# Softmax sums beside a preset epsilon, one-instruction adds and minima along an axis, and a new table of order, in an attention, mixture and feed-forward chain

## The chip, the cores and the metric

The kernel runs on one core of one Trainium2 chip. The metric is the device time of one execution in microseconds (us). Before the change it was 473.57 us, the median of three runs (472.63 to 473.67).

## The reference, cut to what matters

Three layers follow one another. A windowed attention with 32 global rows (batch 4, 8 heads, 512 local and 32 global rows, head dimension 64) feeds four attention experts with a causal mask and a gate over the two best experts, and these feed a feed-forward block whose inputs are mixed with the row before. Every softmax divides by a sum to which 1e-9 is added:

```
def sm(s):
    s = s - np.max(s, axis=-1, keepdims=True)
    e = np.exp(s)
    return e / (np.sum(e, axis=-1, keepdims=True) + 1e-09)
s_g = scale * np.matmul(q_g, k_all.transpose(0, 1, 3, 2))
out_g = np.matmul(sm(s_g), v_all)
...
a_l = sm(s_l)
...
a = np.exp(scores)
a /= a.sum(-1, keepdims=True) + 1e-09
ye = a @ v @ wo[e]
```

## The kernel before, in words

The first stage (some 110 us) is the windowed attention. A step `n` is two heads by half of the local rows, 32 steps in all. `a_qk` (line 290) makes the scores of a step on TensorE (PE, tiles `S`). For each of the four pieces of a step VectorE (DVE) takes the row minimum of the negated scores while it adds the mask (tile `sm`, minimum in `mn`), and ScalarE (ACT) takes the exponential and adds up the rows into a column of `su` (line 316). `a_norm` (line 320) adds EPS to the four sums with a `tensor_scalar` into `rc`, takes the reciprocal, both on DVE, and GpSimd (POOL) multiplies the exponentials by it (tiles `pn`, `glob`). `a_tp` and `a_tg` transpose on PE (`pT`, `pTg`), and `a_pv` multiplies with the values on PE (tiles `x`). The 32 global rows of a batch go the same way in `g_qk`, `g_norm`, `g_tp` and `g_pv` (lines 367 to 422; tiles `Sga`, `Sgb`, `gl`, `pTG`, `pTh`, `xg`); there the minimum of two partial minima is a `tensor_tensor` (line 384), and `g_norm` adds EPS to one sum per half (line 392).

The second stage (to some 250 us) is the experts: projections `pv` and `pb`, scores `C` in `c_qk` (line 560), EPS and reciprocal in `c_norm` (line 581, tile `crc`), a multiplication by the gate and the scaling of `csm` on POOL, transposes `cT`, products `y`. The 32 last rows of a batch go through `l_qk` and `l_norm` (lines 610 and 629). The third stage multiplies the expert outputs with combined weights `G` (tiles `Gr`, `Gk`; `r00c` is the first product with them), then runs `k` and `v` to the end and stores.

Sums stand in small tiles of their own, `su` in 4 rotating buffers, `csu` in 3 and `sug` in 2, written with a step of two elements where a step has several.

Nothing is sent when it is called. `chain_kernel` records every operation in a list (class `Log`), and line 1052 sends them in the order of a table, ORDER: a string of steps, where `-3` goes back three places and `22x6` goes forward 22 and takes six operations in a row. Each engine works in that order, as do the DMA issues on the SP queue, and an instruction that waits holds up what stands behind it on its engine. SLOTS says which of its rotating buffers a tile takes. Both tables were made outside the kernel.

Of the kernel before, what the change touches and what calls it, by code (L numbers as in the profile page):

```python
# [18 lines left out]
S = SL + SG  # L19
# [100 lines left out]
def chain_kernel(ctx: ExitStack, tc: tile.TileContext, kq, vw, vgd, wqkv, wo, pack, w_k, w_v, w_r, c_causal, out):  # L120
# [30 lines left out]
    mu = small[:, SG + B + 144:SG + B + 144 + 2 * NC].rearrange("p (k c) -> p k c", k=2)  # L151
    zcol = tiny.tile([128, 1], F32, name="zcol")
# [137 lines left out]
    def a_qk(n):  # L290
# [29 lines left out]
    def a_norm(n):  # L320
# [6 lines left out]
        nc.vector.tensor_scalar(rc, su, EPS, None, op0=ALU.add)  # L327
# [39 lines left out]
    def g_qk(b):  # L367
# [9 lines left out]
        for h in range(2):  # L377
            t = pg[h]
            mn = T("mng", [4], f"mng{b}{h}", F32, 2)
            su = T("sug", [1], f"sug{b}{h}", F32, 2)  # L380
# [3 lines left out]
            nc.vector.tensor_tensor(mn[:, 2:3], mn[:, 0:1], mn[:, 1:2], op=ALU.min)  # L384
            nc.scalar.activation(t, t, AF.Exp, bias=mn[:, 2:3], scale=-1.0, accum_out=su)
            rs["g", b, h] = su

    def g_norm(b, h):
# [3 lines left out]
        nc.vector.tensor_scalar(rc, su, EPS, None, op0=ALU.add)  # L392
# [167 lines left out]
    def c_qk(b, ep, i):  # L560
# [5 lines left out]
        su = T("csu", [2, 2], f"csu{b}{ep}{i}", F32, 3)[:, :, 0]  # L566
# [4 lines left out]
        for e in range(2):  # L571
# [4 lines left out]
                                            accum_out=su[:, e:e + 1])  # L576
# [4 lines left out]
    def c_norm(b, ep, i):  # L581
# [3 lines left out]
        nc.vector.tensor_scalar(rc, su, EPS, None, op0=ALU.add)  # L585
# [24 lines left out]
    def l_qk(b):  # L610
# [8 lines left out]
        su = T("lsu", [1], f"lsu{b}", F32, 1)  # L619
# [6 lines left out]
        nc.scalar.activation(t[:, 0:S], t[:, 0:S], AF.Exp, bias=mn[:, 3:4], scale=-1.0, accum_out=su)  # L626
        crs["l", b] = su

    def l_norm(b):
# [4 lines left out]
        nc.vector.tensor_scalar(rc, su, EPS, None, op0=ALU.add)  # L634
# [420 lines left out]
def sequence(text):  # L1055
    n = 0
    for word in text.split():
# [8 lines left out]
0 10 -3 9 -19x2 22x6 -7 -15 7 -16 13 -12 -3 10 -11 16 -15 -2 4 3 -3 -2 585 -486 -95 65x8 -29x8 21 1 -2 2 -76 209x8  # L1066
-141 -4 -77 51 25 -25 65 -65 23 -23 438 -472x8 21 164 1 -164 101 64 -65 -106 -24 128 -124 -6x2 1 132 -119 110 -28x8 79
-182 -3 68 54 -55 -75 74 32x8 -143x8 21 113 -63 21 59 3x8 -11 -21 -131 150 32 -88x8 -111 190 -55 29 -94 83 -152 -6 -2
61 105 23 -56 -75 -61 71x8 56 121 -167 74 -33 -137 61 -61 174x4 31 -150 106 35 6 -175 141 32 -15 1 -163 -20 116 65 -54
-42 -47 74 171 -204 -68 45 -3 2 -47 172 44 295 -476 63x4 -106 547 -376 95 -124 -107 204x4 263 -444 180 -145 -56x4 196  # L1070
-230x4 1686 -1539 -120 -30 44 67x4 106 -107 36x32 338 -423 -86 226 -232 231 -206 -26 230 5x4 -214 447 -388 153 -32x8
22 1 230 -386 -5 92x8 -103 8 155x8 -175 9 100 -164 158 -18x2 -83 134 -195 189 -3 6 56x8 -168 70 -22 -50 70 27 -99 64
31 170x8 -215 33 72 -168 164 -99 75x4 24 -171 167 -72 -27 146x40 -112 -100 22 100x2 107 -212 103 207 -106 -205x4 91
174 -85 -83 101 -272x4 332 -282 320 -308 70x4 14 9 98 -16 -249 139 -47x4 65 -6 122x8 -40 -152 222 187 -172x8 165 -459
456 -189 -199 -76 70 50x32 -85 393 -388x2 -6x2 202 -199 -9 232 -225 217 -77 77 -146x2 145 -85 -138 121 -129 126 -121
133 32x8 -34 51 -31 -88 65 18 3 -21 -71 99x8 202 -192 -36 83x8 -87 -43 260 -218 -44 262 -204 -38x4 12 149 -153 26 196
-74 -174 49 -46 40 -149x5 193x4 180x12 -192 -95 1386 -1343 69 -3 -68 69 -6 325x12 -332 -38 26 178 -206 -76 107 3 -44
# [201 lines left out]
```

## Time and profile before

| | us |
|---|---|
| median of three runs | 473.57 |
| lowest and highest | 472.63, 473.67 |
| the profiled execution's own time | 474.15 |
| its span, first to last instruction | 472.4 |
| what lies around the span | 1.75 |

The profile is of one execution. Busy times are of instructions; a matmul's end is modelled, since matmuls are pipelined, so a busy PE isn't PE at its peak. The chain of waits is followed back from the last instruction: at each step to what released it, or to the instruction ahead of it on its engine. Idle time is put down to what ended it.

### The profile page before, as it was taken

Reading aid. Unit: us, or ns where it says so; the run is one execution under the profiler, and the core shown is the slowest. Engines: PE = TensorE matmul, PEld = TensorE weight load, DVE = VectorE, ACT = ScalarE, POOL = GpSimd, SP = SyncE. Lnnn points to the kernel's source line nnn. Section 1 sums busy time; section 2 is a strip of 40 time slices with the busy share of each in tenths; the row PEclk is TensorE's granted clock in tenths of the full one; section 3 lists DMA queues with packets and bytes.
Section 4 is the critical chain, followed back from the end, with each engine's and each line's share of the span. In section 5 each row is a group of like instructions: output and inputs, shape, how many; then the busy total and the mean of one; then the engine's idle time right before and its main releaser. Section 6 shows DMA issues by size and latency. Waiting matters only on the chain.

```text
span 472.4 us, 11799 instructions
## 1 busy us (share of the span) xinstructions
PE 460.1 (97%) x4226; PEld 394.4 (83%) x4226; DVE 340.8 (72%) x1170; ACT 293.7 (62%) x917; POOL 277.7 (59%) x439
## 2 busy tenths in 40 slices
PE   8799999999999999999999999999999999999996
PEld 6688788989997998897768768898888988889884
DVE  4799878967798577887799979999973652238512
ACT  5999899876767666777677867865440423215230
POOL 4989677486457777963897337665551244305450
PEclk9899999999999999999999999999999999999999
DMA  8978373201100000102121654422523500015003
GB/s 328 411 293 316 117 267 145 92 25 46 46 3 1 2 0 2 46 2 89 46 67 47 211 191 164 142 60 61 149 74 111 180 2 0 1 54 177 17 0 111
DMA packets 19701, 48.38 MB, mean 102 GB/s; under 512 B 2484, under 2 KB 3124, under 8 KB 19644
## 3 DMA queue, kind: packets, MB, share of 16 engines
q1 hardware_dynamic: 19356, 47.38, 29.8%
q8 instruction: 33, 0.54, 0.5%
q10 hardware_dynamic: 288, 0.26, 0.2%
q14 instruction: 24, 0.20, 0.1%
HBM read 38.70 MB, written 8.93 MB: 101 GB/s over the span
## 4 chain that ended last, share of the span: by engine, by line
PE 79%; DVE 7%; POOL 5%; ACT 4%; DMA 3%; issue 1%; ACTq 0%; POOLq 0%; DVEq 0%
PE v L107 20%; PE x L107 5%; PE pv L107 4%; PE S L107 4%; PE y L107 3%; PE C L107 3%; PE pT L107 3%; PE cT L107 3%; POOL csm L107 2%; PE Gr L107 1%; PE xg L107 1%; DVE csm L107 1%; DMA rawk<-in_moe_w_k_dram 1%; DMA rawv<-in_moe_w_v_dram 1%; ACT sm L107 1%
## 5 line engine op out<-in xcount | busy, mean ns | idle before, releaser
L107 PE MATMUL v<-wv,kk 128*128 128x512 f32 x408 | 99.3, 391 | 0.0
L107 PEld LDWEIGHTS v<-wv,kk 128*128 128x128 f32 x408 | 74.1, 188 | 13.7 <-POOL kk L107 0.2
L107 ACT ACTIVATE sm<-sm,mn 128x160 f32<-128x160 f32 x128 | 53.4, 421 | 7.4 <-DVE mn L107 7.3
L107 POOL TENSOR_TENSOR kk<-kb,kk 128x512 fp32r<-128x512 f32 (+3 forms) x40 | 34.7, 885 | 38.1 <-ACT kk L107 37.8
L107 POOL TENSOR_TENSOR csm<-csm,crc 128x512 f32<-128x512 f32 (+3 forms) x64 | 46.8, 752 | 1.2
L107 POOL TENSOR_TENSOR pn<-sm,rc 128x256 f32<-128x256 f32 x64 | 39.1, 631 | 13.2 <-DVE rc L107 8.6
L107 ACT ACTIVATE csm<-csm,cmn 128x384 f32<-128x384 f32 (+3 forms) x64 | 35.9, 562 | 15.4 <-DVE cmn L107 11.6
L107 DVE CUSTOM_DVE_ANT_0 sm<-S,band 128x160 f32<-128x160 f32 x128 | 35.6, 315 | 10.3 <-PE S L107 7.3
L107 POOL TENSOR_TENSOR kk<-kd,kk 128x256 fp32r<-128x256 f32 (+2 forms) x32 | 20.3, 644 | 36.8 <-ACT kk L107 36.8
L107 DVE CUSTOM_DVE_ANT_0 csm<-C,causal 128x384 f32<-128x384 f32 (+3 forms) x64 | 30.6, 485 | 8.3 <-PE cT L107 3.5
L107 DVE SCALAR_TENSOR_TENSOR kb<-kc,ks 128x256 f32<-128x256 f32 (+1 forms) x24 | 16.8, 699 | 21.0 <-ACT ks L107 17.2
L107 DVE TENSOR_TENSOR ro<-v,ro 128x512 f32<-128x512 f32 x17 | 11.6, 690 | 27.7 <-PE v L107 27.7
L107 POOL TENSOR_TENSOR x<-xT,x 128x256 fp32r<-128x256 f32 (+1 forms) x32 | 24.0, 777 | 8.6 <-ACT x L107 7.7
L107 PE MATMUL pv<-wv,x 128*128 128x260 f32 x192 | 26.9, 289 | 0.0
L107 PE MATMUL cT<-ident,csm 128*128 128x128 f32 x160 | 25.3, 277 | 1.1 <-POOL csm L107 0.7
L107 PE MATMUL S<-kq 64*64 64x160 f32 x512 | 24.1, 322 | 1.6 <-DMA kq<-in_kq_dram 1.0
L107 PEld LDWEIGHTS S<-kq 64*64 64x64 f32 x512 | 18.0, 142 | 7.9 <-issue 3.8
L107 DVE SCALAR_TENSOR_TENSOR kd<-kd 128x256 f32<-128x256 f32 (+1 forms) x24 | 14.1, 591 | 14.5 <-ACT kd L107 14.4
L107 PEld LDWEIGHTS pv<-wv,x 128*128 128x128 f32 x192 | 24.2, 189 | 0.5 <-ACT xT L107 0.2
L107 ACT ACTIVATION_READ_ACCUMULATOR sm<-sm,mn 128x1 f32 x128 | 24.4, 190 | 0.0
L107 ACT CAST kk<-kb 128x512 fp32r<-128x512 f32 (+3 forms) x40 | 16.0, 438 | 11.2 <-PE v L107 8.4
L107 PE MATMUL C<-qk 64*128 64x512 f32 (+3 forms) x192 | 22.7, 349 | 0.0
(908 smaller groups left out, 1335.9 us busy)
## 6 DMA issues: line engine op xcount, KB each, us to landing
kq<-in_kq_dram SPq DMA_DIRECT2D x15, 688.0 KB, 7.4
vw<-in_vw_dram SPq DMA_DIRECT2D x16, 512.0 KB, 8.0
rawk<-in_moe_w_k_dram SPq DMA_DIRECT2D x16, 256.0 KB, 3.4
rawv<-in_moe_w_v_dram SPq DMA_DIRECT2D x16, 256.0 KB, 3.0
ro<-rd SPq DMA_DIRECT2D x16, 256.0 KB, 3.5
rd<-rt SPq DMA_DIRECT2D x15, 256.0 KB, 3.8
rawr<-in_moe_w_r_dram SPq DMA_DIRECT2D x4, 512.0 KB, 4.9
out_dram<-ro SPq DMA_DIRECT2D x7, 256.0 KB, 2.0
```

Source lines behind the costliest of these rows:

```text
L107: getattr(getattr(self.nc, engine), name)(*[now(x) for x in args], **{k: now(x) for k, x in kwargs.items()})
```

## The change

Two tiles that last for the whole kernel, `sums` and `csums`, are filled with EPS by two memsets on POOL. Each sum is now written into the first of two elements, and EPS stays in the second. Adding EPS becomes a sum over that pair: in `a_norm`, `g_norm`, `c_norm` and `l_norm` a `tensor_reduce` takes the place of the `tensor_scalar` (32, 8, 32 and 4 instructions), and in `g_qk` a `tensor_reduce` over the two partial minima takes the place of the `tensor_tensor` (8 instructions). No instruction is taken away, and the two memsets are added.

ORDER and SLOTS are new. All 5,607 old operations are in the new table, most of them at another place.

```
+    sums = tiny.tile([128, 16, 4, 2], F32, name="sums")
+    nc.gpsimd.memset(sums, EPS)
+    csums = tiny.tile([128, 28, 2, 2], F32, name="csums")
+    nc.gpsimd.memset(csums, EPS)
...
-        su = T("su", [4, 2], f"su{n}", F32, 4)[:, :, 0]
+        su = sums[:, n % 16]
...
-                                                accum_out=su[:, c:c + 1])
+                                                accum_out=su[:, c, 0:1])
...
-        nc.vector.tensor_scalar(rc, su, EPS, None, op0=ALU.add)
+        nc.vector.tensor_reduce(rc, su, AX.X, ALU.add)
...
-            su = T("sug", [1], f"sug{b}{h}", F32, 2)
+            su = csums[:, 16 + 2 * b + h, 0]
...
-            nc.vector.tensor_tensor(mn[:, 2:3], mn[:, 0:1], mn[:, 1:2], op=ALU.min)
-            nc.scalar.activation(t, t, AF.Exp, bias=mn[:, 2:3], scale=-1.0, accum_out=su)
+            nc.vector.tensor_reduce(mn[:, 2:3], mn[:, 0:2], AX.X, ALU.min)
+            nc.scalar.activation(t, t, AF.Exp, bias=mn[:, 2:3], scale=-1.0, accum_out=su[:, 0:1])
...
-        su = T("csu", [2, 2], f"csu{b}{ep}{i}", F32, 3)[:, :, 0]
+        su = csums[:, (8 * b + 4 * ep + i) % 16]
...
-        su = T("lsu", [1], f"lsu{b}", F32, 1)
+        su = csums[:, 24 + b, 0]
...
 ORDER = """
-0 10 -3 9 -19x2 22x6 -7 -15 7 -16 13 -12 -3 10 -11 16 -15 -2 4 3 -3 -2 585 -486 -95 65x8 -29x8 21 1 -2 2 -76 209x8
...
```

Read out of the two tables, with the names of the tiles (S is both heads of a step, Sg all of `Sga` and `Sgb` of a batch):

```
DMA issues on SP, old: kq1, kq3, kq0 (2 parts), kq2, wq, vw0, vgb, vw1, small, wv, vw, vw, kq4, kq5, kq6
DMA issues on SP, new: kq1, kq3, kq2, kq0 (2 parts), wq, vw0, vw1, vw2, vw3, vgb, small, kq4, wv, kq5, kq6

PE, old: six warming matmuls; S3 S2 S7 S1 Sg0 S0 S6 S5 S4 pT3 pT2 pTG00 pTh00 pT1 pT0 pTg0
         x00 x01 (first values) pTG01 pTh01 S9 S8 S10
PE, new: S3 S2 S7, six warming matmuls; Sg0 S0 S1 S4 S5 S6 pTG00 pTh00 pTG01 pTh01 pT3 pT7 S9
         pT1 pT0 pT2 pTg0 S8 S10 S11 x00 x01

POOL near 245 us, old: crc x2, csm x4, then Gr x2, Gr0d x2; new: csm, Gr, crc, csm x2, Gr0d x2 (the other
         Gr stands ahead of crc311)
PE near 245 us, old: cT3130 cT3131 cT3100 cT3101 y311 y310 r00c; new: cT3130 cT3111 cT3131 r00c cT3100 cT3101 y311 y310
```

## Rows read from the trace of the kernel before

**Rows 1.** The page: busy us, share of the span and instructions of each engine.
```profile
PE 460.1 (97%) x4226; PEld 394.4 (83%) x4226; DVE 340.8 (72%) x1170; ACT 293.7 (62%) x917; POOL 277.7 (59%) x439
```

**Rows 2.** Busy time of each engine in three stretches, with granted clock and DMA.
```profile
core 0: us, PE busy (x) PEld busy (x) DVE busy (x) ACT busy (x) POOL busy (x), PEclk, DMA share, GB/s
0.00:12.00 12.00, 9.94 (x132) 7.51 (x136) 5.52 (x39) 6.36 (x25) 5.29 (x21) 1.00 0.86 328
12.00:24.00 12.00, 9.28 (x143) 7.55 (x132) 9.60 (x57) 11.73 (x46) 12.00 (x21) 0.86 1.03 413
...
96.00:240.00 144.00, 143.21 (x1377) 124.66 (x1372) 113.32 (x439) 100.63 (x302) 99.02 (x176) 1.00 0.08 25
```

**Rows 3.** Chain that ended last: by engine, then pieces (start us, us, what) before 21 us.
```profile
PE 79%; DVE 7%; POOL 5%; ACT 4%; DMA 3%; issue 1%; ACTq 0%; POOLq 0%; DVEq 0%
...
15.92 0.59 DVE rc L107
...
17.18 0.38 DVE mng L107
```

**Rows 4.** What PE waited for: us in total, times, longest.
```profile
PE pTG L107 <- POOL gl L107: 1.6, 1, 1.6
...
PE cT L107 <- POOL csm L107: 0.7, 2, 0.4
PE S L107 <- DVE mn L107: 0.7, 2, 0.5
```

**Rows 5.** DVE groups by shape: busy us, mean ns of one, idle before.
```profile
L107 DVE CUSTOM_DVE_ANT_0 sm<-S,band 128x160 f32<-128x160 f32 x128 | 35.6, 315 | 10.3 <-PE S L107 7.3 <-ACT sm L107 1.8 <-POOL pn L107 1.0
...
L107 DVE TENSOR_SCALAR crc<-csu 128x2 f32<-128x2 f32 x32 | 8.7, 286 | 2.1 <-ACT csm L107 2.0
...
L107 DVE TENSOR_SCALAR rc<-su 128x4 f32<-128x4 f32 x32 | 8.5, 278 | 4.2 <-ACT sm L107 4.2
...
L107 DVE TENSOR_TENSOR mng<-mng 128x1 f32<-128x1 f32 x8 | 1.7, 224 | 0.0
...
L107 DVE TENSOR_SCALAR rcg<-sug 128x1 f32<-128x1 f32 x8 | 1.1, 144 | 0.0
...
L107 DVE TENSOR_REDUCE gs<-gd 128x4 f32<-128x16 f32 x4 | 0.6, 160 | 0.0
...
L107 DVE TENSOR_REDUCE lmn<-lmn 128x1 f32<-128x3 f32 x4 | 0.6, 156 | 0.0
```

**Rows 6.** Instructions on tile rc: ns min/median/max, first and last start.
```profile
L107 DVE TENSOR_SCALAR rc<-su x32: 139/168/1268, 9.2 to 102.9; 128x4 f32<-128x4 f32 x32
```

**Rows 7.** Timeline of DVE and POOL at 23 and at 144 us: start, us, what.
```profile
23.28 1.44 POOL L107 TENSOR_TENSOR wv<-rawwv,wv 128x260 fp32r<-128x260 f32 x2
23.48 1.27 DVE L107 TENSOR_SCALAR rc<-su 128x4 f32<-128x4 f32 x1 [1.99 <-ACT sm L107]
...
143.74 1.19 POOL L107 TENSOR_TENSOR csm<-csm,crc 128x256 f32<-128x256 f32 x2
...
143.91 0.16 DVE L107 TENSOR_REDUCE lmn<-lmn 128x1 f32<-128x3 f32 x1
```

**Rows 8.** Timeline of POOL and PE in the first 21 us.
```profile
0.73 0.20 POOL L107 MEMSET ident<- 128x128 f32 x1 [0.29 <-POOLq L1263]
...
9.64 1.18 PE L107 MATMUL Sga<-kq 64*32 64x512 f32 x12
...
17.59 0.66 PE L107 MATMUL pTG<-ident,gl 128*128 128x128 f32 x4 [1.57 <-POOL gl L107]
...
20.95 2.94 PE L107 MATMUL x<-pt,vw 128*64 128x64 f32 x64 [0.19 <-ACT pt L107]
```

**Rows 9.** Timeline of POOL and PE at 244 to 250 us.
```profile
245.14 1.09 PE L107 MATMUL cT<-ident,csm 128*128 128x128 f32 x6 [0.36 <-POOL csm L107]
...
245.81 2.69 POOL L107 TENSOR_TENSOR Gr<-g0r,Gr 128x512 fp32r<-128x512 f32 x2
...
249.43 0.74 PE L107 MATMUL r00c<-Gr,dH 128*128 128x512 f32 x2
```

More of the change, by code (lines that the diff above doesn't have):

```diff
@@ L391, in g_norm @@
         rc = T("rcg", [1], f"rcg{b}{h}", F32, 2)
-        nc.vector.tensor_scalar(rc, su, EPS, None, op0=ALU.add)
+        nc.vector.tensor_reduce(rc, su, AX.X, ALU.add)
         nc.vector.reciprocal(rc, rc)
@@ L584, in c_norm @@
         rc = T("crc", [2], f"crc{b}{ep}{i}", F32, 3)
-        nc.vector.tensor_scalar(rc, su, EPS, None, op0=ALU.add)
+        nc.vector.tensor_reduce(rc, su, AX.X, ALU.add)
         nc.vector.reciprocal(rc, rc)
@@ L633, in l_norm @@
         rc = T("lrc", [1], f"lrc{b}", F32, 1)
-        nc.vector.tensor_scalar(rc, su, EPS, None, op0=ALU.add)
+        nc.vector.tensor_reduce(rc, su, AX.X, ALU.add)
         nc.vector.reciprocal(rc, rc)
@@ new lines @@
+92 -119 94 182 -156 6 151 20x8 -12 -212 226 -14 32 -23 -230 226 -140x40 125 -122 -5 101 2 -48x8 -61 61 -254x4 95 157
+-323x4 65 98 277 -318 124 64 -153 155 -320 280x8 -18x2 60 -206 134 -11 -100 112 -174x4 167 -137 -32 37x4 129 6x4 -140
+132 -6 -21 17 -18 24 5 92x8 -111 170 -167 -12 246 -176 14 29 3 -33 155 2 -127 -96 3 -125x32 89 -90x2 116 32 155 -179
+-11 -34 6 34 -39 29 -34 64 27 59x8 -64 -183 118 151x8 -278 306 -189 -32 220 -350x4 344 -199 138 -130x4 59 63 62 -347
+188x4 27 3 56 -88x4 27 -66 60 -29 92 -89 179x12 -168 1268 -1205 -62 -77 1342 -953x12 -163 -205 27 12 163 -164 1263
@@ new lines @@
+-1281 16 422x12 -446 1275 -1318 106 -98 100 290x8 -352x32 55 341 830 -943 -272 -95 476 -797 353 99 -10 -48x2 51 3 -10
+2 -3 4 3 -37 264 -261x4 -29 20 8x4 23 -29 -29 20 12 27x4 -19 -13 31 -46 10 267x8 -241 253 -300 294 -253 10x8 -419
+455x8 191 -655 562 -563 32 583x8 -202 -390 -34 417 -39 179 -145 2x2 155x8 -550 434 -46 -2 46 -46 228 -7 -134x40 -520
+381 377 -375 168 -118 1077 -926 -36 -6 -159 239x12 -14 -112 99 -32 42 -38 -3 -4 -38 -2 4 -9 -29 5x12 19 157 -72 -31
+-94 38 -8 162 -72 71 -169 43 -339x4 279 -146x4 218 -77 -105 210x8 -257 -139 176 457x8 -190 -118 -206 322 -60 -64 64
@@ new lines @@
+113 -52 -63 -154x12 15 239 -114 14 -2 47 -47 155 -353 352 -94 12x2 79 -58 57 -23x3 -298 259 -38 -99x12 271 -408 296 19
+-82 171 -251x12 59 179 -183 2 -8 186 -186 174x4 -176 -93 33 119x3 -156 257x4 -228 121 117 -188 78x6 90 14x6 -242 132
+100 -240 192x6 -60 -87 193 -247 246 -48 87x6 -55 -82x12 28 2 46 -50 -202 6 -5 228 -225 242 5x12 -265 293 -127x2 125
+-295 294 -292 291 -198x12 -106 163 121 5 -34 33 -128 93 26 -121 126 -294 197x12 52 -3 -156 155 1 -263 322 -323 322
+-323 160 161 -221 220 -280x2 244x12 -96 -85 -77 160 -85 200 -136x2 -116x12 104 110 -111 110 -111 -126 241x6 13 -261x2
@@ new lines @@
+-34 -157 162 -160 173x6 -20x2 -163 1x2 35 123 378 -172 -218x6 4 -161 539 -503 122 21 355 -501 501 -242x6 36 -153x2
+-30x2 28 162 -172x6 352 -349 -168 165 174 2 171 -514 164 348 -238x6 56 135 -310 -166 165 172 -26 -80x6 -34 107 -4 12
+-13 -100x6 106 -154 153x2 12 -162x6 143 12 -13 12x2 -14 -90x6 97 -160 288 -283 288 -137 -160x6 1x2 294 -144 128 -280
+-2 280 -51x12 39 -238 -44 280 -281 298 -19 2 -284 280 3 -2 1 -72x12 64 -5 -49 52 -35 34 -54 53 -7 6 -55 57 -280 280
+-110x12 92 -8 -262 -2 269 -267 210 16 148 -380 354 -83 -282x6 5 227 -56 55 -232 269 -39 -59 98 -61 -64x12 14 56 128
@@ new lines @@
+-89 -59 58 -61 18 135 -136 -22 3 -201x6 193 137 -179 178 -354 292x12 49 -180 -175 214 143 -185 199 -22 -178 183 -186 1
+440x6 -270 -51 -127 333x6 -159 -341 341 -36x12 -159 175x2 -331x2 275 1 -278 368 -36 -343x6 14 -12 309 35 29 -30 -14
+-334 346 -99x12 73 13 -347 -2 366 -366 332 33 -2 -21 21 -22 -14 34 -356x6 315 37 -38 33 161x6 -164 -355 354 -5 -35
+148x6 -116 -39 17 181 -512 844 -534 -319x6 278 -33 -245 -2 278 -34 -245 413x6 -73 -101 -247 507x6 -513 245 -4 72 136
+59x6 -194 -325 242 -243 343 113x6 -139 -81 99 -22 -78x12 67 137 367 -362 -471 470 44 -515 323 88 56 -472 325 41 -56
@@ new lines @@
+151x3 50x3 -206 240x3 -286x2 287x3 -249 -42 41 450 -198x3 -298 41 327 -185x3 -188 375 -49 41x6 -375 271 -232 286 73x6
+-132 -4 -272 234x3 -237 286x3 -16 51 -326 320 -45x3 46 49 -376 325x3 -8 54 -340 291x6 -297 299x3 -302 -39 38 300x3
+-342 476 -439 -39 347x6 46 -362 239x3 -272 357 -329 328 37x6 -39 75 -76 -44x3 -324 401 -44 30x6 -395x2 357 42x6 -406
+361x3 46 -47x3 38 -406 405 -40x3 -369 409 -36x3 508 -481 4 -43x3 40 -6 -36x3 33 308x6 -59x6 -257x21 236 -234x3 -5 8x3
+-11 13x3 -5 8x3 -6 -6 13x3 -5 -7x2 55x6 -51 -6 214x6 196 -412 1x6 -7 213 6 -214x6 -7 415 -222x6 -237 243x6 1x2 212
@@ new lines @@
+-20 -4 51 -39x3 164x6 -82 -53 4x3 -7 54 -55 8x3 120 -82 87 -139 10x3 -9x3 46 154x6 -267 183x6 77 -215 12x3 130x2
+-132x3 35x21 17x3 -19 71 1 -66x3 61 -54 -20 73 -74x4 7 7x4 -18 6x2 13x3 -6 -19 235x6 -217 -7 117x6 -123 5 41x6 411
+-343 6 -20x6 340 -404 273x6 145 -349x2 139x6 194 -340 -73x6 376 -307 -3 -2 311 -433x6 47 376 -371 49x6 8 -105 243 -143
+-69x6 -39 348x6 -307 -48 47 82x6 -135 1 -4 352 56 -393x6 26 -3 359 -161x6 -252 46 -12x2 146x6 -188 249 -215 10 190x6
+-206 1 -4 213x6 99x6 -96 -10x3 -221 141 85 26x6 -202 -58 320 -264 88x6 175 -268 -3 2 259x6 -268 92 -76x6 253 -177 -2
@@ new lines @@
+-7x6 178 -255 77 -147x3 72x6 -84x3 147 -67 211x6 -151 2 -3 -68x6 225 -162 161 -79 -87 -95x3 184x6 -96x2 -161x3 160 -3
+2 -109x3 103 -68 -99x3 94 17x3 -19 158x7 -209x3 273 1 -11 8 -222x3 211 8 -8 -4 -220 -95x3 92 -40x3 256 -228 228 -226
+160 -142x3 -17 -10x2 163 -159 12x3 143 -163 -44x3 46 -9 64x3 -62 164x2 -105x3 53x3 -6x3 -109x3 53x3 45 -7 3 2 -44x3 34
+-6 8 -8 21x3 -26 -37x3 35 67x3 -16 5 -6 8x3 -15 8 -6 5 13x3 -26 -37x3 37 5 59x3 23x3 -32x3 30 3x3 -6x2 -24x6 23 -6 5x2
+-91x3 67 -15x3 12x2 18x3 -21 -133x3 130 20 -21 -79x3 96x2 -45x3 42x3 1x2
@@ L1182 @@
     ),
     "csm0": (
[L1184 to L1190 removed]
+        "032034113024021340223100022413424321042431032042213013422243120034123244131044401304320132103421"
@@ L1191 @@
+        "0312140232332401042310110234012342043232243104204310324100200134042"
+    ),
+    "mn": "00200121201011201020102011210221",
+    "wy": "010101010111001110001101111101010",
+    "rc": "02102011201021200120122021212011",
     "csm1": (
-        "021020112001120210012020021111101202122200211202210200012210100111012012010200120212000210021002"
-        "21021021210220210221101002211002101012102110"
+        "021020112010122001201120210202111021021120122001102112100021110200210210210211020200101021200210"
+        "21120120010112020112200120202102020101022012"
@@ L1194 @@
     ),
-    "cpt": "10010110010010100110100110",
+    "cpt": "10010101011001101001101001",
     "mng": "01011001",
-    "sug": "01101001",
-    "wg": "010000011011110000101101000010110",
-    "rcg": "01101001",
-    "qk": "100120010210210222222210",
+    "wg": "010000011101110000100010000110110",
+    "rcg": "01011001",
+    "qk": "101021110120120111111102",
     "lg": "0000",
     "gate2": "0101",
-    "cmn": "02010211202111100222211001200121",
-    "csu": "21020212200110122100210210211020",
-    "crc": "02101021101010211202112002102210",
+    "cmn": "21201020012220010121220110210021",
@@ L1206 @@
+    "crc": "01200121201202012100102120120012",
 }
```

189 lines of the change are left out of this document (72 added, 117 removed).

## The prediction

> **What bounds the kernel now.** I read the busy times first: PE is busy for 97% of the span, DVE for 72%, ACT for 62%, POOL for 59% [rows 1]. A PE that is busy by its records may still be late, so the second view is by stretches. From 96 to 240 us PE is busy for 143.21 of 144 us while DVE has 31 us to spare [rows 2]: there a faster DVE instruction is worth next to nothing unless a PE wait hangs on it. The first 24 us are different. PE is busy for 9.94 and 9.28 us of 12, ACT for 11.73 of the second 12 and POOL for all of them, and DMA runs at a share of 0.86 and 1.03: PE is fed too slowly [rows 2]. The third view, the chain that ended last, agrees: 79% of it is PE, 7% DVE, and of the edited instructions the two largest pieces lie before 21 us, 0.59 us of `rc` and 0.38 us of `mng` [rows 3]. The last view is what PE waits for. Its three largest waits for DVE or POOL after the first microsecond are 1.6, 0.7 and 0.7 us, 3.0 us in all [rows 4]. That is the most that relief on these two engines alone can hand to PE by its recorded waits.
>
> **Part 1: the adds and minima.** The `tensor_scalar` takes 278 ns on `rc` and 286 on `crc`, on four and two elements, but 144 on `rcg`, one element [rows 5]. Size can't be the reason: on `rc` the fastest is 139, the median 168, the slowest 1268 ns [rows 6]. The slowest started at 23.48 us, just after POOL had begun a pair of subtractions at 23.28, and it ended at 24.75 as that pair did, at 24.72 [rows 7]. So DVE's instruction stood still until POOL's was through. A `tensor_reduce` at 143.91 us ran in its usual 0.16 us wholly inside POOL work of 143.74 to 144.93 [rows 7]: it isn't held.
>
> Its price: the rows have 160 ns for 16 elements in and 4 out and 156 for 3 in and 1 out [rows 5]. The new ones read 8, 4 or 2 elements, so I take 160; the bounds are 156 and, should they be held as well, the 278 and 286 of now. On `rc` that saves 32 x (278 - 160) = 3.8 us, on `crc` 32 x (286 - 160) = 4.0, on `mng` 8 x (224 - 160) = 0.5. On `rcg` it costs 8 x (160 - 144) = 0.1, and as little on the four of `l_norm`. DVE's busy time falls by 8.2 us (0 to 8.5 by the bounds).
>
> [...]
>
> How much of the 8.2 us reaches PE? Nearly all stands beside PE work that fills 99% of the stretch [rows 2]; were that cover gone, all 8.2 would count. What is left is the start, where the chain runs through 0.59 us of `rc` and 0.38 of `mng`: without the hold, 0.43 and 0.22 less [rows 3]. ACT is as full there, so not all of it arrives. I take -0.5 us; bounds 0 and -3.0, the waits above.
>
> **Part 2: the tiles.** Two memsets of 128 x 128 and 128 x 112 go to POOL; one of 128 x 128 takes 0.20 us [rows 8]. They stand among the first instructions, and POOL has 5.29 busy us in the first 12 [rows 2]. Cost 0; if POOL's masks came late, 0.4. The buffers of the sums no longer turn: before, the exponential of step n + 4 could wait for the `tensor_scalar` of step n. No such wait has a row, so 0.
>
> **Part 3: the table at the start.** This is the largest unknown. The old order begins `x00` at 20.95 us [rows 8]. The new one has, before `x00`, all that stood there plus `pT7`, `pTG01`, `pTh01` and `S9`: nine transposes, at most 9 x 0.165 = 1.5 us (four in 0.66, a pipelined end included [rows 8]), and the score matmuls of one step; I put them together at an estimated 1.6 us of work taken from later. Against that, `rc0` and `rc2` on DVE stand behind the four `sm6` minima, 4 x 315 ns = 1.26 us [rows 5], and POOL's `pn0`, `pn2` and PE's `pT0`, `pT2` wait for them. That leaves -0.4 us. On SP, `kq0` goes behind `kq2`, and `Sg0` needs all four `kq` in both orders, as before at 9.64 us [rows 8]; `vw2` and `vw3` now precede `kq4`, which `S9` needs. Bounds for the walk: -1.6 (nothing of the delay) to +1.3 (all of the delay, none of the work counts).
>
> **Part 4: the clock.** [...]
>
> **Part 5: the rest of the table.** The same matmuls run, in 566 runs of one tile against 565, so PE's own work stays. The one move that I could price is near 245 us: `r00c`, 6 x 0.23 us, goes ahead of the last transposes, where PE waits for `csm` (0.36 us [rows 9]). But it needs both `Gr` on POOL, 1.35 us each, of which one now stands in front of the last `csm` [rows 9]: the hole moves, and I count 0 (bounds -1.1, the hole filled, and +1.4, the `csm` that much later). The loads for `Gk` keep nearly their order: 0, bounds -1 and +1.
>
> **Sum.** -0.5 + 0 - 0.4 - 0.8 + 0 = -1.7 us. The profiled execution took 474.15 us, its span 472.4 and 1.75 around it; 474.15 - 1.7 = 472.45. The median of the runs is 0.58 lower, so **471.9 us**.
>
> **Rivals.**
> *No change.* PE's work is the same and covers DVE; the time saved in one wait comes back in the next, since ACT and POOL are full at the start (11.73 and 12.00 of 12 [rows 2]). For it: 143.21 of 144. Against: 3.0 us of PE waits [rows 4]. Parts 3 and 4 at zero and part 1 between 0 and -0.5: 473.3 us. Chance 0.26. A change that doesn't do what it says (the pair sum is held by POOL too) ends here as well; the one row of an unheld `tensor_reduce` of three elements [rows 7] is against it.
> *Slower: the start starves.* `Sg0` now stands on PE ahead of S0, S1, S4, S5 and S6, and its last `kq` comes last on a queue already full (413 GB/s [rows 2]). If `kq0` lands later than about 10.5 us, DVE has taken all twelve minima of S3, S2 and S7 and idles, ACT behind it; from there each microsecond is one at the end. [...] Chance 0.17. Against it: two parts of `kq0` are issued by ACT and come early.
> *Much faster.* [...] Part of the first chance; 0.05.
>
> **The numbers.** A measurement of this kernel can tell about 0.2%, 0.95 us. Forecast (with the case above) 0.57, no change 0.26, slower 0.17. The forecast's own range is 470.3 to 472.6 (parts 3 and 4 each a microsecond better or worse). The range for 8 in 10 adds no change and the half of the slower case: 469.7 to 475.0.
>
> **What would show it.** In the new profile the pair sums should stand at 150 to 170 ns each with no long ones, and DVE's busy time some 8 us lower. The first 24 us should show PE busier and a clock above 0.86. 96 to 240 us should look as before. `r00c` should start near 246 us with the last `cT` behind it. I am wrong if pair sums of 0.3 us and more remain, if the clock row has a second slice below 1.00, or if `Sg0` starts well after 10 us.

## The result: 476.95 us, slower by 0.8%

The kernel after takes 476.95 us (median of 11 runs, 475.88 to 481.46), the kernel before 473.57 (472.63 to 476.12). The ratio is 1.0077 with an interval of 1.0049 to 1.0104. The forecast was 471.9 us, its range ended at 475.0. The profiled execution of after took 476.65 us, its span 474.7.

The sums of busy time show none of the loss. The page of after has, in answer to [rows 1]:

```profile
PE 456.2 (96%) x4226; PEld 390.8 (82%) x4226; DVE 332.1 (70%) x1170; ACT 293.1 (62%) x917; POOL 275.4 (58%) x441
```

DVE does 8.7 us less than in [rows 1], as forecast. The groups of DVE by shape, in answer to [rows 5], and the instructions on tile `rc`, in answer to [rows 6]:

```profile
L107 DVE TENSOR_REDUCE crc<-csums 128x2 f32<-128x4 f32 x32 | 4.5, 150 | 2.7 <-ACT csm L107 2.0 <-POOL csm L107 0.3
...
L107 DVE TENSOR_REDUCE rc<-sums 128x4 f32<-128x8 f32 x32 | 4.3, 153 | 1.0 <-ACT sm L107 0.8 <-POOL glob L107 0.2
L107 DVE TENSOR_REDUCE mng<-mng 128x1 f32<-128x2 f32 x8 | 1.1, 148 | 0.0
L107 DVE TENSOR_REDUCE rcg<-csums 128x1 f32<-128x2 f32 x8 | 1.0, 137 | 0.0
```

```profile
L107 DVE TENSOR_REDUCE rc<-sums x32: 122/152/163, 10.2 to 104.4; 128x4 f32<-128x8 f32 x32
```

Not one of the 32 sums is held any more: the longest takes 163 ns, where it took 1268. The windows of after answer to [rows 2]; 24 to 48 us is added, and under it the same stretch of before:

```profile
core 0: us, PE busy (x) PEld busy (x) DVE busy (x) ACT busy (x) POOL busy (x), PEclk, DMA share, GB/s
0.00:12.00 12.00, 7.03 (x100) 5.23 (x104) 3.62 (x29) 6.10 (x23) 4.96 (x21) 1.00 0.86 326
12.00:24.00 12.00, 8.61 (x130) 6.77 (x122) 10.60 (x75) 11.74 (x50) 11.88 (x21) 1.00 1.03 413
24.00:48.00 24.00, 22.01 (x453) 17.43 (x452) 19.14 (x113) 21.87 (x85) 18.58 (x33) 1.00 0.78 294
96.00:240.00 144.00, 143.69 (x1481) 126.17 (x1474) 111.84 (x456) 100.25 (x304) 99.27 (x179) 1.00 0.10 33
```

```profile
24.00:48.00 24.00, 24.00 (x436) 19.74 (x436) 21.96 (x118) 23.37 (x94) 20.94 (x36) 1.00 0.77 298
```

From 24 to 48 us PE is busy for 22.01 us where it was busy for all 24.00. The missing 1.99 us are two stops of 0.89 and 1.10 us. PE's waits name them, in answer to [rows 4], and the timeline of PE shows where they stand:

```profile
PE S L107 <- DMA kq<-in_kq_dram: 5.7, 2, 4.9
PE pTG L107 <- DVE rc L107: 1.1, 1, 1.1
PE x L107 <- issue: 1.1, 1, 1.1
PE r10a L107 <- ACT rc L107: 0.9, 1, 0.9
PE Sgb L107 <- issue: 0.9, 1, 0.9
PE Gk L107 <- DVE g0k L107: 0.8, 1, 0.8
PE k12a L107 <- DVE ro L107: 0.7, 1, 0.7
...
PE pTG L107 <- POOL gl L107: 0.5, 1, 0.5
```

```profile
32.75 0.25 PE L107 MATMUL Sgb<-kq 64*32 64x32 f32 x3
33.88 0.28 PE L107 MATMUL Sgb<-kq 64*32 64x32 f32 x13 [0.89 <-issue]
...
38.10 1.96 PE L107 MATMUL x<-pt,vw 128*64 128x64 f32 x59
41.17 0.34 PE L107 MATMUL x<-pt,vw 128*64 128x64 f32 x5 [1.10 <-issue]
```

"issue" is a time for which no releaser shows. The stops stand in the middle of a tile, behind its 3rd matmul of 16 and its 59th of 64, where all operands and the bank are the same as for the matmul ahead. So a late operand is unlikely as the reason. Everything that PE has in the trace is a record here: matmuls, weight loads, its sequencer's own. Counted from the start, the first stop lies behind record 961 and the second behind record 1217: 256 apart. And the trace has a queue "q8 instruction" with 33 packets of 16 KB in the whole span. Here are the DMA views of after for three stretches: one packet of that queue and nothing else, then none for 6 us beside four loads of `kq` and two of `vw`, then one again:

```profile
DMA packets 1, 0.02 MB, mean 15 GB/s; under 512 B 0, under 2 KB 0, under 8 KB 0
...
q8 instruction: 1, 0.02, 5.5%
```

(31.5 to 32.6 us; the packet runs from 31.55 to 32.52)

```profile
q1 hardware_dynamic: 303, 1.35, 68.9%
issues: line engine op xcount, KB each, median us to landing
kq<-in_kq_dram SPq DMA_DIRECT2D x4, 688.0 KB, 8.0
vw<-in_vw_dram SPq DMA_DIRECT2D x2, 512.0 KB, 8.3
```

(32.6 to 38.8 us)

```profile
q1 hardware_dynamic: 70, 0.32, 88.3%
q8 instruction: 1, 0.02, 5.9%
```

(38.9 to 40.0 us; the packet runs from 38.93 to 39.98)

PE goes on 1.36 us after the first of them has landed and 1.19 us after the second. My reading was that PE had run out of instructions. The experiments had to show it, and also whether these stops are the loss at all: if each matmul is given the usual time of its form in before (the median from its start to the next start), and the time passed is compared with the work done, after is some 3.0 us behind before at 50 us, 0.4 at 245 us and 2.8 at the end. By that count the loss could as well have lain behind 245 us.

### The profile page after: what moved, and what is told of

The parts are those of the page before. It is cut to its first block, busy times and chain, and to the rows that moved or that the text cites. A ratio compares the mean times of both kernels' runs of the same rounds, so it can differ in the third digit from the quotient of the medians.

```text
span 474.7 us, 11815 instructions
## 1 busy us (share of the span) xinstructions
PE 456.2 (96%) x4226; PEld 390.8 (82%) x4226; DVE 332.1 (70%) x1170; ACT 293.1 (62%) x917; POOL 275.4 (58%) x441
## 4 chain that ended last, share of the span: by engine, by line
PE 73%; DVE 10%; DMA 5%; POOL 5%; ACT 4%; issue 2%; SPq 1%; POOLq 0%; DVEq 0%; ACTq 0%
PE v L107 19%; PE x L107 5%; PE pv L107 4%; PE S L107 4%; PE C L107 3%; PE y L107 3%; PE pT L107 3%; PE cT L107 3%; POOL csm L107 2%; DMA rawk<-in_moe_w_k_dram 2%; DVE yk L107 2%; DVE rawk L107 2%; ACT sm L107 1%; PE Gr L107 1%; PE xg L107 1%
## 5 line engine op out<-in xcount | busy, mean ns | idle before, releaser
L107 PE MATMUL v<-wv,kk 128*128 128x512 f32 x408 | 96.8, 391 | 0.0
L107 PEld LDWEIGHTS v<-wv,kk 128*128 128x128 f32 x408 | 75.1, 188 | 14.4
L107 POOL TENSOR_TENSOR csm<-csm,crc 128x128 f32<-128x128 f32 (+3 forms) x64 | 47.6, 766 | 1.1
L107 ACT ACTIVATE csm<-csm,cmn 128x512 f32<-128x512 f32 (+3 forms) x64 | 35.9, 561 | 11.0 <-DVE cmn L107 10.3
L107 DVE CUSTOM_DVE_ANT_0 csm<-C,causal 128x512 f32<-128x512 f32 (+3 forms) x64 | 29.8, 485 | 6.9 <-PE C L107 2.1
L107 POOL TENSOR_TENSOR x<-xT,x 128x256 fp32r<-128x256 f32 (+1 forms) x32 | 25.1, 810 | 3.2 <-ACT x L107 1.8
L107 PE MATMUL cT<-ident,csm 128*128 128x128 f32 x160 | 23.4, 277 | 0.8 <-POOL csm L107 0.6
L107 POOL TENSOR_TENSOR wv<-yv,wv 128x256 fp32r<-128x256 f32 x16 | 14.3, 894 | 16.2 <-ACT wv L107 13.8
L107 POOL TENSOR_TENSOR crc<-crc,gate 128x2 f32<-128x2 f32 x32 | 6.4, 211 | 26.9 <-DVE crc L107 23.6
```

The costliest lines, as they stand in the source:

```text
L107: getattr(getattr(self.nc, engine), name)(*[now(x) for x in args], **{k: now(x) for k, x in kwargs.items()})
```

## The experiments

Three theories stood at first. A: the new order costs, behind 245 us. B: the exchange of instructions costs. C: the new order costs at its start. Where two orders are joined, the first so many instructions are those of one table and the rest are what is left, in the other's order; buffers are assigned anew where they must be. The diffs of orders are shorthand for other strings in ORDER and SLOTS. "new" and "old" are the two tables, and all edits of the change are in, unless something else is said. Every run gives its ratio to runs of before beside it on its own chip; the runs are spread over several chips, so two of them are compared by these ratios rather than by their medians.

**1. The edits in the old order.**

```diff
-        nc.emit(new)
+        nc.emit(old + the two memsets behind POOL's masks)
```

> All the edited instructions and the two persistent tiles, but in the order of the kernel before; the two memsets stand on POOL behind the masks. Theory A (the new table is what costs, and it costs behind 245 us: the profiles of before and after stand level there, PE is then 1.6 us later by 305 us and 0.9 us more at 375 us; the exchange of instructions alone gains a little): 471.5 to 473.2 us, DVE busy some 8 us less than before. Theory B (the exchange itself costs, since DVE or ACT now run into something else): 475 to 477 us. Theory C (the table costs at the start, where PE stood still within xg, Sgb and x between 30 and 45 us, and what is lost there is lost for good): as A here, 471.5 to 473.2 us.

Measured: 473.00 us, ratio 0.9984 (0.9970 to 0.9998). DVE is busy for 335.8 us. B falls: the exchange of instructions is a small gain, 0.8 us by the ratio.

**2. The old instructions in the new order.**

```diff
-        nc.vector.tensor_reduce(rc, su, AX.X, ALU.add)
+        nc.vector.tensor_scalar(rc, su[:, :, 0], EPS, None, op0=ALU.add)
...
-            nc.vector.tensor_reduce(mn[:, 2:3], mn[:, 0:2], AX.X, ALU.min)
+            nc.vector.tensor_tensor(mn[:, 2:3], mn[:, 0:1], mn[:, 1:2], op=ALU.min)
```

> The kernel after with its table, its tiles and its buffers, but with the old instructions on them: tensor_scalar on one column of the sums, tensor_tensor for the minimum. Theory A and C (the table costs): as slow as after or slower, 476.5 to 478.5 us, with holes on PE at 290 to 305 and at 375 us as after has them. Theory B (the exchange costs): 473 to 474 us.

Measured: 478.59 us, 1.0095 (1.0068 to 1.0123), with stops of 1.26 us in `Sgb` and 1.38 in `x`. That is 0.1 us above the range of A and C, and far from B: the table costs, with either set of instructions. DVE is busy for 337.6 us, 5.5 more than in after in the same order, so the longer time goes with the instruction.

**3 and 4. The table in two halves, cut near 246 us.**

```diff
-        nc.emit(new)
+        nc.emit(new[:3650] + rest in old)
...
+        nc.emit(old[:3640] + rest in new)
```

> All edits; the new order for the first 3650 instructions, to about 246 us, and from there on what is left in the old order. Theory A (the loss lies behind 245 us): 472.5 to 474.5 us, since after stood level with before at 245 us. Theory C (lost at the start): 475.5 to 477 us. Theory B: 475 to 477 us.

> All edits; the old order for the first 3640 instructions, to about 246 us, and from there on what is left in the new order. Theory A: 474.5 to 476.5 us, with the holes at 290 to 305 and at 375 us. Theory C: 471.5 to 473.5 us. Theory B: 475 to 477 us.

Measured: 477.33 us, 1.0081 (1.0063 to 1.0099) with the new order first, and 473.67, 0.9994 (0.9977 to 1.0010) with the old one first. A falls, C stands (both runs lie 0.2 to 0.3 us outside its ranges), although after's profile was nearly level with before's at 245 us: the two executions taken alone misled me. By the ratios the order ahead of 245 us costs 0.97%, 4.6 us, and the one behind it 0.1%, which the intervals don't tell from nothing. The third run has the stops at the same two matmuls; the fourth and the first have no stop of 0.15 us or more without a releaser:

```profile
34.38 0.29 PE L107 MATMUL Sgb<-kq 64*32 64x32 f32 x13 [1.14 <-issue]
41.94 0.34 PE L107 MATMUL x<-pt,vw 128*64 128x64 f32 x5 [1.38 <-issue]
```

**5. The new order for its first 26 us alone.**

```diff
+        nc.emit(new[:320] + rest in old)
```

> All edits; the new order for the first 320 instructions (to S11, about 26 us), then what is left in the old order. In the traces so far the kernels with the new order at the start are 1.7 us late by 25 us against those with the old one, and lose 2.5 us more in two holes inside Sgb and x between 32 and 42 us. Theory S+D (both count, the holes come from the order behind 26 us): 474 to 475.2 us, no hole of 0.5 us without a releaser. Rival S (the start breeds the holes too): 476 to 477.5 us. Rival D (only the holes count, the start is absorbed): 472.5 to 473.5 us.

Measured: 474.64 us, 1.0006 (0.9978 to 1.0035), no stop, as S+D said. Against run 1 the start costs 1.0 us by the ratios; the intervals overlap, so neither its size nor its sign is certain, and it is the smaller part of the 4.6 us.

**6. The old start before the new middle.**

```diff
+        nc.emit(old[:350] + new to 245 us + rest in old)
```

> All edits; the old order for the first 350 instructions (to about 27 us), then the new one to about 246 us, then the old one. Theory S+D: the two holes are there, 474.5 to 476 us, or a little less if the table's middle (130 to 245 us), in which the new order caught up by 1.7 us, keeps that gain. Rival S: no holes, 471.5 to 473.3 us. Rival D: 475 to 476 us.

Measured: 481.87 us, 1.0163 (1.0145 to 1.0182), and no stop without a releaser. The join has waits of its own (`S` for DVE's `mn` 2.2 us in three waits, for ACT's `xT` 1.0), so it says little of either table: a miss for all three expectations.

**7. The loads beside the second stop.** Theory D, from the 256 records between the two stops and the packets of q8 that land 1.36 and 1.19 us before PE goes on: PE's instructions come in blocks of 256, and a block that lands late stops PE.

```diff
 vw6, vw6
-kq8, kq11, kq9, kq10
+kq10, kq8, kq11, kq9
```

> The kernel after, but on SP the three loads kq8, kq11 and kq9 stand behind kq10, so that they leave at 38 us and later in place of 34 to 36 us. Theory D (PE stands still within x because its next block of 256 instructions is fetched behind these loads: every hole without a releaser lies at a block's end, and PE goes on 1.2 to 1.6 us after that block's packet has landed): the packet that started at 38.9 us starts at 36 to 37 us, the hole in x (1.10 us) goes, the one in Sgb stays, and the time is 475.5 to 476.3 us. Rival (the hole has another cause, a wait that the records do not name): the hole stays in x and the time is 476.7 to 477.3 us.

Measured: the packet of 38.93 us starts at 36.90, the stop in `x` is gone, that in `Sgb` stays: as D said. But the time is 480.44 us, 1.0147 (1.0118 to 1.0177), since PE then waits 4.15 us at 45.59 for a `kq`. The price of the delay was not in my expectation. The waits of PE:

```profile
PE S L107 <- DMA kq<-in_kq_dram: 9.1, 2, 4.9
PE pTG L107 <- DVE rc L107: 1.2, 1, 1.2
PE Sgb L107 <- issue: 1.1, 1, 1.1
```

**8. The blocks shifted.** 32 small matmuls, which nothing reads, stand ahead of everything, where PE has nothing to do until 4.9 us. They add 128 instructions and so move the ends of all blocks by half a block; the order of the work is that of after.

```diff
-            for _ in range(6):
-                nc.tensor.matmul(st[0][:, 0:128], warm, warm, start=True, stop=True)
+            for k in range(38):
+                w, m = (128, 128) if k < 6 else (32, 16)
+                nc.tensor.matmul(st[0][0:w, 0:m], warm[:, 0:w], warm[:, 0:m], start=True, stop=True)
```

> The kernel after with 32 small matmuls (32 columns of weights, 16 of data, 64 records) put ahead of the first one, where PE has nothing to do until 4.9 us; nothing else is moved. Theory D (blocks of 256 instructions): both holes move 64 matmul records up the program, the first out of Sgb into xg, the second out of x into the score matmuls ahead of it; the time stays within 1 us of after. Rival (another wait at these tiles): the holes stay behind the 3rd matmul of Sgb and the 59th of x.

Measured: 473.95 us, 0.9995 (0.9981 to 1.0010), against 1.0077 for after. Both stops are gone, and the time with them: D had them move and the time stay within 1 us, the rival had them stay, so neither forecast came true. From 24 to 48 us PE is full again:

```profile
24.00:48.00 24.00, 23.93 (x472) 19.67 (x473) 21.43 (x120) 23.99 (x97) 21.05 (x37) 1.00 0.76 298
```

The count also says whose queue q8 is: after has 8,590 records of PE, 33.55 times 256, and 33 packets on q8; this run has 8,718, 34.05 times 256, and 34 packets. Before has 8,584, 33.53 times 256, and 33 packets. One packet stands to each whole block of 256 in these three.

**9. A smaller shift:** 8 small matmuls, an eighth of a block (the diff is that of run 8 with `range(14)`).

> As the run with 32 small matmuls ahead of everything, but with 8 of them (16 matmul records, 32 instructions, an eighth of a block). Theory D (PE's instructions come in blocks of 256, and a block that lands late stops PE at its first instruction): holes, where there still are any, lie 16 matmul records further up than in after, in xg behind its 67th matmul and in x behind its 43rd; the time is between that of 32 small ones (473.95 us) and of after (476.95 us). Rival (the wait belongs to the tiles Sgb and x, and the 32 small ones helped by keeping PE's clock or its start busy): holes behind the 3rd of Sgb and the 59th of x again, or none with a time near 474 us.

Measured: 475.35 us, 1.0023 (1.0004 to 1.0042). The two old stops are gone, and there is one new one of 1.68 us at an earlier block's end, record 705, in another tile's middle:

```profile
27.82 0.75 PE L107 MATMUL x<-pt,vw 128*64 128x64 f32 x20
30.25 0.45 PE L107 MATMUL x<-pt,vw 128*64 128x64 f32 x8 [1.68 <-issue]
```

The time lies in D's range, the place that I gave was wrong, and the rival fell too: the stop doesn't belong to the tile; it stands where a block ends. It lasts until 1.55 us after its packet has landed.

**10. One load moved past the fetch.**

```diff
-rawr0, vw4, vw4
+vw4, vw4, rawr0
```

> The kernel after with one load moved: on SP the 512 KB of rawr0 stand behind the two loads of vw4 in place of ahead of them, 1.6 us later; nothing needs them before 45 us. Theory D with a queue (the fetch of the block that starts near 26.8 us waits behind the loads issued before it; 512 KB are 1.25 us at the 410 KB per us that the queues then move): that packet starts near 25.5 us, the next near 30.3, the hole in Sgb goes, the one in x goes or shrinks, and the time is 474 to 475.8 us. Rival (the fetch does not queue behind the loads): packets and holes as in after, 476.5 to 477.3 us.

Measured: 477.47 us, 1.0046 (1.0018 to 1.0075). The packet of 26.77 us starts at 26.77 again: it was not queued behind `rawr0`, as the rival said, and the time is 0.2 us above the rival's range. The next but one starts at 37.91 in place of 38.93, and the stop in `x` shrinks to 0.28 us.

**11. The shift in the old order.** Run 1 with the 32 small matmuls behind the six that warm.

> All edits in the old order (473.0 us), with the 32 small matmuls behind the six that warm. There the blocks were in time up to 65 us, where two packets left the least slack seen (1.4 to 1.5 us) and PE a hole of 0.26 us. Theory D: no hole of 0.5 us either way, 472 to 473.5 us. Rival (the small matmuls help in themselves, by the clock or by filling PE): 3 us less as in the new table, 470 to 471 us.

Measured: 474.49 us, 1.0002 (0.9976 to 1.0027). That is 1 us above D's range, and level with before. Without long stops to remove the small matmuls bring nothing; so in run 8 it was not they themselves that helped.

**12 and 14. The first loads in the old order,** beside the 32 small matmuls and without them.

```diff
-kq2, kq0, kq0, rawwq, vw0, vw0, vw2, vw2, vgb, small, kq4, rawwv, kq5, kq6, kq7
+kq0, kq0, kq2, rawwq, vw0, vw0, vgb, small, kq4, rawwv, kq5, kq6, kq7, vw2, vw2
```

> The new table with the 32 small matmuls (473.95 us), and on SP the first loads in an order like the old one: both pieces of kq0 ahead of kq2, and vw2 behind kq7, so that kq4 leaves earlier. Theory S (the new table's first 26 us cost 1.6 us because kq0 and kq4 land late: there Sga waits 0.8 us for kq and S9 in after 0.8 us): 472.3 to 473.4 us, Sga without a wait for a load. Rival (what the start costs comes from the order on DVE and ACT): 473.6 to 474.6 us.

> The kernel after with, on SP, both pieces of kq0 ahead of kq2 and vw2 behind kq7; no small matmuls. Theory D (blocks of instructions are fetched behind the loads): the packet that started at 26.8 us starts 1 us or more earlier, as it did by 4.6 us when the same loads were moved beside the small matmuls, the next follows, the hole in Sgb (0.9 us) goes, that in x may stay (its packet meets the loads of kq8 to kq11), 475 to 476.2 us. Rival (only the place of the blocks counts): both holes as in after, 476.6 to 477.4 us.

Measured: 473.59 us, 0.9980 (0.9962 to 0.9999) with the small matmuls, and 476.75, 1.0050 (1.0026 to 1.0074) without. With them `Sga` waits 0.4 us for `kq` in place of 0.8, and the gain over run 8 lies within the scatter. Without them both stops are there, 1.15 and 1.38 us, and the packet of 26.77 us starts at 27.49. So the order of the first loads neither breeds the stops nor cures them. The place of the blocks does: between these two runs, which differ by the small matmuls alone, it is worth 0.70%, 3.3 us, a second time.

**13. The new order for 12 us alone.**

```diff
+        nc.emit(new[:133] + rest in old)
```

> All edits; the new order for the first 133 instructions (to S1, about 12 us), then what is left in the old order. If the 1.6 us that the new order costs by 26 us arise in the first 12 us (kq0 and the global scores late, the warming matmuls behind S7): 474.2 to 475.2 us. If they arise between 12 and 26 us (the order of minima, exponentials and transposes): 472.6 to 473.6 us.

Measured: 477.68 us, 1.0069 (1.0049 to 1.0088), outside both. PE waits 3.73 us there for DVE ahead of `pTG`, where after waits 1.12 us and before not at all: the join is the likely cause, and the run doesn't answer its question.

**15. The mended new order to 246 us, the old one behind it.** Run 12 to 246 us, then old.

> The run with the first loads moved and 32 small matmuls (473.59 us) to about 246 us, and the old order from there on. If the new order behind 245 us costs the 0.7 us that it cost behind the old start: 472.6 to 473.2 us, at the level of the edits in the old order (473.0). If the middle of the new order gains besides, as the kernels that came late into it seemed to show (1.7 us between 50 and 240 us): 471 to 472.5 us, faster than both. If neither: 473.3 to 474 us.

Measured: 473.97 us, 0.9992 (0.9975 to 1.0010): neither the table's end nor its middle is worth anything that shows.

**16. A piece of POOL taken out of the chain.** Run 8, and on POOL:

```diff
-wq, glob0, pn0, pn0, pn2, pn2, glob0
+glob0, pn0, pn0, pn2, pn2, glob0, wq
```

> The new order with 32 small matmuls (473.95 us), and on POOL the third subtraction for wq (0.73 us at 20.64) stands behind pn0, pn2 and their glob. Theory P (POOL's queue sets when pT2, and behind it x00, can start): pT2 starts 0.5 to 0.7 us earlier than at 24.07, x00 than at 26.88, and the time is 473.2 to 473.6 us, a difference as large as the scatter, so the two starts decide. Rival (ACT or DVE stand right behind POOL): pT2 and x00 start within 0.2 us of 24.07 and 26.88.

Measured: 473.63 us, 1.0000 (0.9983 to 1.0016); `pT2` starts at 23.96 us in place of 24.07, and `x00` at 26.71 in place of 26.88. POOL now waits itself, for a transpose that makes its buffer free:

```profile
21.01 0.40 POOL L107 TENSOR_TENSOR glob<-sm,rc 128x128 f32<-128x128 f32 x1 [0.42 <-PE pT L107]
```

Both starts lie within the rival's 0.2 us. Something else stands right behind that piece of POOL, and what the start costs has no single owner that I found.

## Why the prediction was wrong

**The step that failed** is in part 5: "The same matmuls run [...] so PE's own work stays." The matmuls do stay, but by the count of run 8 PE's instructions come in the 33 packets of q8, and that the forecast did not price. I read [rows 2] from 0 to 24 and from 96 to 240 us and priced moves near 245 us, and the stops lie in between, at 33 and 40 us. The term of part 5 was 0; the runs showed long stops of PE where a block of 256 of its instructions ends, behind records 961 and 1217 in after. The stops add up to 1.99 us in the profile of after, and to 2.5 in that of run 3. Shifting the blocks (run 8 against after) is worth 0.82% by the ratios, 3.9 us (2.4 to 5.3 by the two intervals). What lies above the 2 us of the stops themselves is not settled. Compared start by start of the same matmul, after is 0.7 us ahead of run 8 at 33 us, 1.7 us behind at 42, 1.1 behind from 100 to 240, and 2.8 behind at the end. So more than half of the difference of these two executions arises behind 240 us, in the same order of work; there run 8 is spared the wait of 0.7 us for `ro` and half of the 0.8 for `g0k`, and no run shows whether the stops lead to these waits. In runs 14 and 12 it is otherwise: run 14 is 2.9 us behind at 240 us and 2.5 at the end.

Why there? The table gives blocks at whose end PE stops and some where it doesn't, from the records of PE and of the queue q8 (us; a block is entered when its first record starts).

| kernel, records of the block | entered | last record ahead of the stop, or next block | next packet | stop |
|---|---|---|---|---|
| after, 706 to 961 | 29.24 | 32.80 | 31.55 to 32.52 | 1.08 |
| after, 962 to 1217 | 33.88 | 39.84 | 38.93 to 39.98 | 1.33 |
| run 7, 962 to 1217 | 34.08 | 40.04 | 36.90 to 37.89 | none |
| before, 706 to 961 | 28.29 | 33.12 | 29.30 to 30.50 | none |
| before, 1986 to 2241 | 62.09 | 65.70 | 63.82 to 64.75 | 0.54 |
| run 8, 706 to 961 | 27.12 | 32.48 | 29.00 to 30.13 | none |
| run 9, 450 to 705 | 21.33 | 28.35 | 27.61 to 28.70 | 1.90 |

(The stop here is from start to start, 0.2 to 0.3 us more than the profile's idle time.) In after the first block holds most of `Sga`, scores and all 80 matmuls of `xg`, which together run in 3.6 us; its successor's packet starts 2.3 us behind the block's beginning, takes 1.0, and PE goes on 1.4 us later: 4.6 us, one more than the block lasts. Before takes 4.8 us over the block of the same number. Further down before has a block as dense, 3.6 us with 80 matmuls of `xg`, and a short stop at its end, five blocks behind record 961, which I had passed over:

```profile
66.24 0.49 PE L107 MATMUL pT<-ident,pn 128*128 128x128 f32 x3 [0.27 <-issue]
```

So a dense block stopped PE in the old order too; there the packet started 1.7 us behind the block's beginning, and the stop stayed short. In the second block the packet starts only 5.1 us behind the beginning, while the loads of `kq` run; with these moved (run 7) it starts after 2.8 us and nothing stops. So my reading is that the one stop comes from density and the other from the loads; run 7 tested the second, and no run thinned out the first block. That the fetch is held up by loads is shown at this place alone: run 10 moved 512 KB from ahead of another packet and it didn't stir. The stop of run 9 isn't dense: its block lasts 7.0 us and its packet starts 6.3 us behind the beginning, with loads at 415 GB/s in the run from 12 to 24 us; whether loads held it was not tried. What sets the moment at which a packet is asked for stays open.

**Part 1, the adds and minima: right.** -0.5 us was said, and run 1 gives -0.8 (-0.1 to -1.4); whether it arises at the start, as I had it, no run shows. The new instructions take 137 to 153 ns for the 160 forecast. DVE's busy time fell by 8.7 us in after and by 5.0 in run 1, for 8.2; the sums themselves take as little in run 1 (154 ns on `rc`, 146 on `crc`), so the 3.7 us between lie in other DVE work. On one element the exchange costs nothing either: `rcg` went from 144 ns to 137.

**Part 2, the tiles: right** at 0, as far as run 1 can tell.

**Part 3, the table at the start: the other sign, as far as measured.** -0.4 was said with bounds of -1.6 and +1.3 (and 1.26 - 1.6 is -0.3); runs 1 and 5 give +1.0, within the bounds and not clear of the scatter, and run 8, which has the new start and no stops, lies 0.11%, 0.5 us, above run 1. The chain of waits of after shows what I had not seen from a list of moved tiles:

```profile
9.14 3.07 ACT sm L107 x14
12.21 0.91 ACT wq L107 x3
13.12 1.48 ACT gl L107 x4
14.59 0.29 ACT wq L107
14.89 3.31 ACT sm L107 x16
...
18.24 1.18 POOL pn L107 x2
...
20.82 1.52 POOL pn L107 x3
...
23.16 0.66 PE pT L107 x4
```

From 9.14 to 18.20 us the chain doesn't leave ACT, which has no gap in that time, and then it runs through POOL to `pT2`. `x00` starts at 25.97 us, where it started at 20.95 [rows 8]: scores and transposes of later steps were put ahead of it. I had priced the DVE instructions ahead of `rc0` and `rc2` (1.26 us), and not that the stretch belongs to ACT. The wait for `gl` did shrink, from 1.57 us [rows 8] to 0.52, but `pTG01` then waits 1.12 us for DVE, which itself has waited 1.19 for ACT.

**Part 4, the clock: the fall is not the table's.** No run shows the -0.8 of the sum. What the fall takes can be read in before: its granted clock is 0.73, 0.50 and 0.50 in the three microseconds from 19 us on and 0.78 in the next two, which adds up to 1.7 us of full clock.

```profile
19.00:20.00 1.00, 0.91 (x6) 0.91 (x7) 0.94 (x8) 1.00 (x5) 1.00 (x3) 0.73 1.05 433
20.00:21.00 1.00, 0.81 (x6) 0.41 (x4) 1.00 (x4) 1.00 (x3) 1.00 (x2) 0.50 1.02 422
21.00:22.00 1.00, 1.00 (x20) 1.00 (x22) 0.49 (x1) 1.00 (x4) 1.00 (x3) 0.50 1.04 429
22.00:24.00 2.00, 2.00 (x52) 1.93 (x49) 0.53 (x1) 1.85 (x10) 2.00 (x5) 0.78 0.99 405
```

After has a granted clock of 1.00 from 12 to 24 us where before had 0.86 [rows 2], which looks like a hit. But run 1, with the old order and a wait of 1.80 us for `gl`, has 1.00 too, and runs 2 and 3, with the new order, have 0.86. Of 18 profiles six have the fall in that stretch, with either order. Run 12, with the fall in its profile, has a median of 473.59 us, and run 8, without, 473.95. I took one execution's clock for a property of the order.

**Part 5, `r00c`: as forecast.** It starts at 246.21 us, and PE waits 0.59 us for the last `csm` there, for 0.36 before: the hole stays. (The lower bound of -1.1 had no row behind it: the hole of [rows 9] is 0.36 us.) The table behind 245 us costs 0.1%, within the scatter.

**The rivals.** The slower one, which I had put at 476.4 us with 1.7 for the clock in it, lies close to the result, but for another reason. Its condition can't be told from the trace, which doesn't show the landing of the last part of `kq0`: `Sga` starts at 10.66 us, right behind the six warming matmuls (from 8.66 us on) and without a recorded wait for a load, and DVE idles 0.89 us for it. The clock did not fall in after (1.00 from 0 to 24 us), and run 12 shows that bringing `kq0` earlier is worth less than the scatter. None of the three cases named PE's own supply, and that is why the range was too short. The forecast's own range of 470.3 to 472.6 doesn't follow from its terms either: parts 3 and 4 each a microsecond worse give 473.9.

**Which version beats both?** The edits in the old order (run 1), 473.00 us, ratio 0.9984 (0.9970 to 0.9998). Run 12, the new order with small matmuls and the old first loads, is level with it: 473.59 and 0.9980 (0.9962 to 0.9999).

## What to carry to other kernels

An exchange of instructions and a new order are two changes: run the exchange in the old order first, since here its gain of 0.8 us was buried under a loss of 4.6. Where many small matmuls stand in a row, look in PE's timeline for idle time without a releaser in the middle of a tile, count the records between two such stops, and compare with the packets of the instruction queue; idle instructions where PE waits anyway can move a block's end off the spot, as 128 of them did in run 8 (another tile between two dense ones might do so too; no run tried it). And a clock that falls in one execution belongs to the order only when another execution of the same order repeats it.

## What was not expected of the hardware

- PE stopped where a block of its instructions ends: 0.83 to 1.68 us at a time behind record 705, 961 or 1217, which are multiples of 256 apart, and it went on 1.2 to 1.6 us after a 16 KB packet of the queue q8 has landed, in all seven kernels that show such a stop (after, runs 2, 3, 7, 9, 10 and 14). Short ones of 0.26 to 0.31 us end so too: behind record 1217 in run 10, 1985 in runs 2 and 14, and 2241 in before.
- 128 idle instructions at the start took 0.8% off a kernel of 477 us (run 8), and nothing off one without the long stops (run 11).
- The granted clock from 12 to 24 us differed between executions that begin with the same program: 1.00 in after, 0.86 in run 3.
